# Last terms of two gate and up halves side by side in 64 rows, with value sums in the maxima banks, in a gated mix of attention and a ReLU-gated block

## The chip, the cores and the metric

The kernel runs on one core of a Trainium2 chip. The metric is the device time of one execution in microseconds; lower is better. TensorE is called PE in the profile, VectorE DVE, ScalarE ACT, GpSimd POOL and SyncE SP.

## The reference

```python
x = A_x                                            # 1 x 2048 x 448
g = sigmoid((x * gate_w).sum(-1, keepdims=True))

# attention: 16 heads of 28
qkv = (x @ wqkv).reshape(B, S, 3, 16, 28)          # q, k, v: b h s d
scores = einsum("bhqd,bhkd->bhqk", q, k) * 28 ** -0.5
a = (einsum("bhqk,bhkd->bhqd", softmax(scores), v)  # heads side by side
     ) @ wo

# gated block on B_x is not used: it reads the same x
gate = einsum("bsd,df->bsf", x, W_gate)            # f = 1792
up = einsum("bsd,df->bsf", x, W_up)
b = einsum("bsf,fd->bsd", gate * (gate > 0) * up, W_down)

out = g * a + (1 - g) * b
```

All inputs and outputs are float32.

## The kernel before

**Terms.** Products that must be precise are made of two parts: a float32 value is split into a high part (fp32r) and the remainder, its low part. A product of x and weights is a sum of high x high, low x high and high x low. The depth is 448: three chunks of 128 rows and one of 64. The 64 rows of the last chunk lie twice in the 128 partitions, for x and for the weights; of the weights, rows 0 to 63 of slot 6 hold the high part and rows 64 to 127 the low part, so one pass gives high and low weights times high x. `TERMS` lists the 11 passes of a product as pairs (slot of weights, chunk of x; chunks 4 to 7 are the low parts of x); `BY_CHUNK` sorts them by chunk, so that the last pass, n = 10, is (6, 7): slot 6 times the low part of x's last chunk. Of that pass only the 64 rows with high weights matter.

**Stages.** First the projections to q, k and v (`qk`, `vproj`), with the first maxima and scores among them. Then 34 rounds of attention, one head after another. At the end a last phase (`todo`, `gate_up`, `wout`, `down`) with the output projection of the heads, the remaining gate and up features, and the down projection.

**A round.** Every engine's order is written out by hand. A round is a string of letters and a number of gate and up halves, `(order, nu)` in `ROUNDS`:

- "s" (`scores`): one pass, 128 keys by 512 queries of scores, in one of two PSUM banks with tag "s"; ScalarE takes the exponential into SBUF, and that frees the bank. In the last three rounds (`LATE`) a pair of "s" goes to a pair of banks with tag "mx" instead (`scores_pair`).
- "m" (`smax`): two passes of scores for the row maxima, some heads ahead, into one of two pairs of banks with tag "mx"; VectorE reduces the pair (`tensor_reduce`, 128x1024).
- "x" (`gu_mm`): one of the 11 passes of a half. Half 0 of a feature is its gate, half 1 its up part, 128 features by 512 rows of x. When a half's passes are done, `relu` (ScalarE) reads the gate, and `spill_h` (VectorE) multiplies the up part by it; GpSimd's queue sends the product to DRAM.

The strings are SHORT (16 s, 8 m, 11 x), LONG (32 s, 16 m, 33 x; 3 halves), WIDE (32 s, 16 m, 44 x; 4 halves) and LATE (32 s, 44 x). There are 25 LONG, 3 WIDE and 3 LATE rounds. After the letters, `split_f` splits the next weights into parts (ScalarE the high parts, GpSimd the low parts), and `pv` makes the value sums of the round's 8 key tiles: per key tile four matmuls in plain float32 with 32 columns each, one for every 512 queries, side by side in the array. A head takes 16 key tiles, so two rounds; its sum stays in the one bank with tag "po" over both, and at the end of the head ScalarE copies it out (`os`), from where the row sums go to DRAM and come back spread (`row_sums`, `spread`) for `normalise`. At the start of every other round `smax_end` transposes a head's maxima ("mt") into the bank with tag "x".

**PSUM** has eight banks: two "s", two pairs "mx", one "po", one "x". In the rounds the halves use the one "x" bank (in LATE the "s" banks, and `relu` runs on VectorE). `ps_any` gives the projections "s", "s", "x" and "po" in turn; the last phase accumulates `down` in the same four and puts gate and up of a feature in a pair of "mx".

**In the last phase** a feature's `gate_up` makes 22 passes in a row; `down`, `wout` and `gate_up` alternate. `done` is the number of features that the rounds have made (50 of 56), so six remain. In `gu_mm`, where the last feature of a block of 512 rows of x has read a chunk for the last time, SyncE's queue reloads that chunk for the next block.

Of the kernel before, what the change touches and what calls it, by code (L numbers as in the profile page):

```python
# [47 lines left out]
ROUNDS = [("ssssssss", 0), ("smssmssmsmss", 0), (SHORT, 1)] + [(LONG, 3)] * 9 + ([(WIDE, 4)] + [(LONG, 3)] * 8) * 2 + [(WIDE, 4)] + [(LATE, 4)] * 3  # L48
NP = 9


# [10 lines left out]
def gated_mix_kernel(ctx, tc, x, wq, wo, wgu, wd, out):  # L62
# [11 lines left out]
    def ps_s(name):  # L74
        return psum.tile([P, TB], F32, tag="s", bufs=2, name=name)
# [16 lines left out]
    def low(dst, src, high):  # L92
        nc.vector.tensor_tensor(dst, src, f32(high), op=OP.subtract)  # L93
# [98 lines left out]
    def xf(tb, b):  # L192
        return X[tb][b // 4][:, b % 4]


    with tc.tile_pool(name="qkv", bufs=1) as pa:
# [61 lines left out]

        def ps_any(name, late=False):
            turn[0] += 1  # L260
            if late:
                return (ps_x, ps_o)[turn[0] % 2](name)
            return (ps_s, ps_s, ps_x, ps_o)[turn[0] % 4](name)

        def mix(n, among):

# [43 lines left out]

        warm = const.tile([P, TB], BF16, name="warm")
        nc.vector.memset(warm, 0.0)
        ps = ps_o("warm_ps")
        for n in range(WARM):
            nc.tensor.matmul(ps, warm[:, :P], warm, start=True, stop=True)

# [104 lines left out]
    def gu_mm(ps, i, s, n):  # L421

        a, b = BY_CHUNK[n]
        nc.tensor.matmul(ps, WS[i][:, s, a], xf(i // NF, b), start=(n == 0), stop=(n == NT - 1))  # L424
# [22 lines left out]


    NI = H * NK
    PO, OS, LS = {}, {}, {}  # L450

    def pv(i):
        h, kt = divmod(i, NK)
        if kt == 0:
            PO[h] = ps_o(f"po_{h}")
        for j in range(NB):
            nc.tensor.matmul(PO[h][32 * j:32 * j + 32], V[:, h // 4 % 2, kt, h % 4], PT[i][:, j], start=(kt == 0),  # L457
                             stop=(kt == NK - 1))
        del PT[i]
        if kt == NK - 1:  # L460
            OS[h] = fe.tile([P, TB], F32, name=f"os_{h}", tag="os", bufs=2)
            nc.scalar.activation(OS[h], PO.pop(h), AF.Copy)
            LS[h] = fe.tile([P, 16], F32, name=f"ls_{h}", tag="ls", bufs=2)
            nc.gpsimd.dma_start(LS[h], OS[h][DH::32].rearrange("j (p c) -> j p c", c=16))

# [35 lines left out]
        act_high(WO[:, 6], r[:, 3])  # L501
        pool_low(WO[64:, 6], r[64:, 3], WO[64:, 6])

    done = sum(n for _, n in ROUNDS) // 2
    nxt = parts = i0 = 0

    def small_things(u):
# [24 lines left out]
    for r, (order, nu) in enumerate(ROUNDS):  # L532
        ni = order.count("s") // NB
        late = order == LATE
        todo = list(range(nxt, nxt + nu))
        nxt += nu
        small_things(i0 // 4)
        if m % (2 * NK) == 0 and i0 <= NI - LEAD:
            smax_end(m // (2 * NK) - 1)
        if late and wor is None:  # L540
            wor = load_wo()
        ns = nx = 0
        for o in order:
            if o == "s":
                i, j = i0 + 1 + ns // NB, ns % NB
                if ns == 4 * NB:
                    small_things(i0 // 4 + 1)
                if len(EARLY) <= i * NB + j < NI * NB and not late:
                    scores(i, j)
                elif late and i < NI and j % 2 == 0:  # L550
                    scores_pair(i, j)
                ns += 1
            elif o == "m":
                smax(m)
                m += 1
            elif nx < NT * nu:
                i, half = divmod(todo[nx // NT], 2)
                if nx % NT == 0:
                    ps = (ps_s if late else ps_x)(f"gu_{i}_{half}")
                gu_mm(ps, i, half, nx % NT)  # L560
                nx += 1
                if nx % NT == 0:
                    spill_h(i, ps) if half else relu(i, ps, late)

        ready = nxt + (ROUNDS[r + 1][1] if r + 1 < len(ROUNDS) else 2)
# [6 lines left out]
        for i in range(i0, i0 + ni):  # L572
            pv(i)
            if i == NI - NK // 2:
                split_wo(wor)
        i0 += ni
    assert i0 == NI and m == len(maxima), (i0, m)
    stk.close()

# [80 lines left out]
    def down(i):  # L660
        tb, f = divmod(i, NF)
        if f == 0:
            ACC[tb] = [ps_s(f"acc_{tb}_0"), ps_s(f"acc_{tb}_1"), ps_x(f"acc_{tb}_2"), ps_o(f"acc_{tb}_3")]
# [82 lines left out]
```

## Time and profile before

| | us |
|---|---|
| median of 3 runs | 1302.82 (1302.03 to 1303.94) |
| the profiled execution | 1303.31 |
| its span in the trace | 1301.5 |
| busy: TensorE | 1293.8 |
| busy: VectorE | 800.2 |
| busy: ScalarE | 759.8 |
| busy: GpSimd | 360.4 |
| granted TensorE clock | 0.998 |

The profile's page gives the busy time of each engine, the span in 40 slices, the chain of work that ended last, and groups of instructions. In a group's row stand the line, the engine and the operation, what it writes and reads, "out<-in" with partitions x elements, and the count; after the bar the busy time and the mean duration of one in ns; after the second bar the idle time of the engine just before them, and what ended it. A row of the timeline has the start, the length in us, the engine, the line, the operation and how many were merged into it; in brackets stand the idle time before it and what ended that. A row of the chain of waits in order of time has start, length and what ran. PEld is the loading of weights, which can run under a matmul. Matmuls are pipelined: the length of one is longer than the distance to the next, so distances are taken from starts. A value sum matmul in float32 leaves two records, and its "po<-V" rows are those whose exponentials lie in free parts of the tile V.

### The profile page before, as it was taken

The numbers are of one execution on the slowest core, as the hardware profiler recorded it, in microseconds if no ns is written. First come the engines' busy times: TensorE is split into PE (matmuls) and PEld (weight loads), VectorE is DVE, ScalarE is ACT, GpSimd is POOL, SyncE is SP. The second block draws the span as 40 slices with busy tenths as digits, with TensorE's granted clock in tenths as the row PEclk, the third lists the DMA queues.
The fourth block names the chain that finished last, engine by engine and source line by source line (L and its number), as shares of the span: only waits on it lengthen the run. The fifth ranks groups of instructions, "written<-read, shape, count | busy, mean of one in ns | idle before, by whom it ended". The sixth has DMA issues, their size and how long they took to land.

```text
span 1301.5 us, 17614 instructions
## 1 busy us (share of the span) xinstructions
PE 1293.8 (99%) x6689; PEld 915.4 (70%) x6689; DVE 800.2 (61%) x832; ACT 759.8 (58%) x1387; POOL 360.4 (28%) x496
## 2 busy tenths in 40 slices
PE   9999999999999999999999999999999999999998
PEld 6888666666666666666666666666666566899997
DVE  6577676666767666766667676767676223553332
ACT  6212586667676676767667667676666665222121
POOL 3222113232222232323224222222223444541020
PEclk9999999999999999999999999999999999999999
DMA  9835524142333614141526143241423234634432
GB/s 312 281 154 227 154 72 109 56 114 62 85 94 93 170 58 95 60 90 57 130 71 170 61 97 77 78 95 52 103 64 102 94 97 150 221 95 156 133 111 78
DMA packets 53533, 148.87 MB, mean 114 GB/s; under 512 B 9992, under 2 KB 17096, under 8 KB 48840
## 3 DMA queue, kind: packets, MB, share of 16 engines
q1 hardware_dynamic: 36376, 98.57, 29.1%
q0 software_dynamic: 16928, 48.93, 10.3%
q8 instruction: 53, 0.87, 0.3%
q14 instruction: 32, 0.26, 0.1%
q10 hardware_dynamic: 144, 0.23, 0.0%
HBM read 102.06 MB, written 46.02 MB: 114 GB/s over the span
## 4 chain that ended last, share of the span: by engine, by line
PE 99%; DVE 0%; DMA 0%; issue 0%; ACT 0%; SPq 0%; DVEq 0%; ACTq 0%
PE gu L424 22%; PE sm L149 18%; PE po L457 17%; PE s L175 17%; PE acc L647 11%; PE qk L285 5%; PE v L295 3%; PE wo L603 3%; PE s L186 2%; DMA xr<-x 0%; PE mt L159 0%; DVE W L93 0%; DVE X L93 0%; DVE mx L151 0%; DVE st L93 0%
## 5 line engine op out<-in xcount | busy, mean ns | idle before, releaser
L151 DVE TENSOR_REDUCE mx<-sm 128x1 f32<-128x1024 f32 x512 | 612.7, 1220 | 203.7 <-PE sm L149 202.9
L177 ACT ACTIVATE P<-s 128x512 f32<-128x512 f32 x724 | 414.2, 597 | 117.6 <-PE s L175 86.1
L424 PE MATMUL gu<-X,wg 128*128 128x512 f32 x1232 | 389.7, 396 | 0.0
L175 PE MATMUL s<-Q,K 114*128 114x512 f32 x932 | 361.2, 403 | 0.0
L149 PE MATMUL sm<-K,Q 112*128 112x512 f32 x1024 | 314.3, 396 | 0.2 <-DVE mx L151 0.2
L424 PEld LDWEIGHTS gu<-X,wg 128*128 128x128 f32 x1232 | 233.3, 189 | 47.8 <-issue 0.8
L175 PEld LDWEIGHTS s<-Q,K 114*128 114x128 f32 x932 | 173.5, 188 | 86.4 <-ACT P L177 36.1
L149 PEld LDWEIGHTS sm<-K,Q 112*128 112x128 f32 x1024 | 193.6, 190 | 44.1 <-issue 1.7
L457 PE MATMUL po<-P,V 128*32 128x512 f32 x1600 | 182.8, 597 | 2.0 <-DVE st L93 2.0
L96 POOL TENSOR_TENSOR wg<-wgr,wg 128x384 fp32r<-128x384 f32 x153 | 142.7, 945 | 101.9 <-issue 51.8
L446 POOL DMA_DIRECT2D h_d<-h x56 | 31.7, 566 | 403.2 <-DVE h L440 357.4
L647 PE MATMUL acc<-WD,hh 128*128 128x448 f32 x672 | 140.9, 368 | 0.0
L177 ACT ACTIVATE V<-s 128x512 f32<-128x512 f32 x208 | 119.5, 598 | 28.3 <-PE s L175 18.8
L647 PEld LDWEIGHTS acc<-WD,hh 128*128 128x128 f32 x672 | 126.1, 188 | 12.8
L457 PEld LDWEIGHTS po<-P,V 128*32 128x32 f32 x1600 | 49.6, 110 | 113.3 <-issue 113.3
L87 ACT ACTIVATE hh<-hr 128x512 fp32r<-128x512 f32 x56 | 35.2, 631 | 120.3 <-PE acc L647 120.3
L93 DVE TENSOR_TENSOR hh<-hr,hh 128x512 fp32r<-128x512 f32 x56 | 43.5, 777 | 64.5 <-ACT hh L87 64.5
L285 PE MATMUL qk<-X,W 128*128 128x512 f32 x308 | 78.8, 396 | 0.3 <-DVE X L93 0.2
L285 PEld LDWEIGHTS qk<-X,W 128*128 128x128 f32 x308 | 57.6, 188 | 15.6 <-DVE X L93 1.6
L440 DVE TENSOR_TENSOR h<-gu,rl 128x512 f32<-128x512 f32 x56 | 38.6, 689 | 39.9 <-PE gu L424 24.6
L87 ACT ACTIVATE wg<-wgr 128x384 fp32r<-128x384 f32 x153 | 61.7, 490 | 0.0
L93 DVE TENSOR_TENSOR mh<-mr,mh 16x128 fp32r<-16x128 f32 x16 | 4.5, 279 | 83.6 <-ACT mh L163 83.6
(68 smaller groups left out, 724.9 us busy)
## 6 DMA issues: line engine op xcount, KB each, us to landing
wgr<-wgu SPq DMA_DIRECT2D x56, 512.0 KB
K<-qk_d SPq DMA_DIRECT2D x64, 224.0 KB
Q<-qk_d SPq DMA_DIRECT2D x64, 224.0 KB
h_d<-h POOLq DMA_DIRECT2D x56, 256.0 KB, 2.3
hr<-h_d SPq DMA_DIRECT2D x56, 256.0 KB
qk_d<-st POOLq DMA_DIRECT2D x22, 512.0 KB, 3.2
x_d<-X POOLq DMA_DIRECT2D x6, 1024.0 KB, 5.1
X<-x_d SPq DMA_DIRECT2D x24, 256.0 KB
```

The source lines that it names most:

```text
L87: nc.scalar.activation(dst, src, AF.Copy)
L93: nc.vector.tensor_tensor(dst, src, f32(high), op=OP.subtract)
L96: nc.gpsimd.tensor_tensor(dst, src, f32(high), op=OP.subtract)
L149: nc.tensor.matmul(ps[:, c, :], Q[h][:GD, u * P:(u + 1) * P], K[h % 3][:GD, k0:k0 + TB], start=True, stop=True)
L151: nc.vector.tensor_reduce(MX[h][:, 2 * u + half:2 * u + half + 1], ps, axis=AX.XY, op=OP.max)
L175: nc.tensor.matmul(ps, K[h % 3][:GD + 2, kt * P:(kt + 1) * P], Q[h][:GD + 2, j * TB:(j + 1) * TB], start=True, stop=True)
L177: nc.scalar.activation(PT[i][:, j], ps, AF.Exp, scale=SCALE)
L285: nc.tensor.matmul(ps, W[:, a, c * P:(c + 1) * P], xf(tb, b), start=(n == 0), stop=(n == NT - 1))
L295: nc.tensor.matmul(ps[:, :VC], xf(tb, b)[:, t * P:(t + 1) * P], W[:, a, 2 * D:], start=(n == 0), stop=(n == NT - 1))
L424: nc.tensor.matmul(ps, WS[i][:, s, a], xf(i // NF, b), start=(n == 0), stop=(n == NT - 1))
L457: nc.tensor.matmul(PO[h][32 * j:32 * j + 32], V[:, h // 4 % 2, kt, h % 4], PT[i][:, j], start=(kt == 0), stop=(kt == NK - 1))
L647: nc.tensor.matmul(ACC[i // NF][t][:, :D], HH[i][:, a, t * P:(t + 1) * P], WD[:, f, b], start=(f == 0 and n == 0), stop=(f == NF - 1 and n ...
```

## The change

The last passes of two halves are issued together, each with 64 rows, one in the upper and one in the lower half of the array. For one half of such a pair (the set `SECOND`) the high part of the weights lies in rows 64 to 127, and the low part in rows 0 to 63; `split_f` makes the low part for each half separately. In the 31 LONG, WIDE and LATE rounds the last two halves are held open without their last pass, and a new letter "h" at the end of the string issues both last passes, followed by `relu` and `spill_h`. So the strings have 31, 42 and 42 x and one h. In the last phase `gate_up` makes the 20 other passes of a feature first, and then the two last ones.

Two halves are open at once and need two banks: "po" is given up and "x" has two. The value sums of a round (a visit) now start anew in each round, in the first bank of a pair with tag "mx" (in LATE rounds in an "x" bank). On a head's first visit ScalarE copies them out; on later ones VectorE adds them to the copy in SBUF. There are 34 visits, 16 of them first ones.

The letters of LONG and WIDE stand in another order too. In LONG a score comes five passes after the one before last in 13 places (before: 9), in WIDE in 7 (before: 5).

```diff
-LONG = "ssmmxsxxsxsmxxsxsmsxxsxxsmmsxxsxxsxsmsxxsmsmsxsxxsxmsmsxxxxsmxssxxmsxsmsxxsmsxmss"
-WIDE = "msxxsmsxsxmsxxsxmsxxxxmssmxsxxsxxsmxmssxxxxsxsmsmsxxxxsxsmsxmsxxsxxxsmsmxxxsxsxxxsxmssxmxxss"
-LATE = "ssxxxssxxxssxxxssxx" * 4
+LONG = "mxsmsxxxxxsmsxsmsxxsmsxsmsxxsmxxsmsxsxxsmsxxsxsmxsxsmsxxsmsxsmsxxsmsxsxxsmsmxssh"
+WIDE = "sxxmxmxxsxxmsxxsxsmxxssxmxmxsxxsxxsxsmsxxsmxssxxxsmsxxsmxsmxsxsmxsmsxsxxsmsxxsmsmsxxsxsh"
+LATE = "ssxxxssxxxssxxxssxx" * 2 + "ssxxxssxxxssxxssxx" * 2 + "h"
...
-    def ps_o(name):
-        return psum.tile([P, TB], F32, tag="po", bufs=1, name=name)
-
     def ps_x(name):
-        return psum.tile([P, TB], F32, tag="x", bufs=1, name=name)
+        return psum.tile([P, TB], F32, tag="x", bufs=2, name=name)
...
+    done = sum(n for _, n in ROUNDS) // 2
+    SECOND = {sum(n for _, n in ROUNDS[:r + 1]) - 1 for r in range(len(ROUNDS)) if "h" in ROUNDS[r][0]}
+    SECOND |= set(range(2 * done + 1, 2 * NB * NF, 2))
+
+    def lane(k):
+        return slice(64 * k, 64 * k + 64)
...
             high(w[:, :, 6], wr[:, :, 3])
-            low(w[64:, :, 6], wr[64:, :, 3], w[64:, :, 6])
+            for s in range(2):
+                rows = lane(1 - (2 * i + s in SECOND))
+                low(w[rows, s, 6], wr[rows, s, 3], w[rows, s, 6])
...
     def gu_mm(ps, i, s, n):
         a, b = BY_CHUNK[n]
-        nc.tensor.matmul(ps, WS[i][:, s, a], xf(i // NF, b), start=(n == 0), stop=(n == NT - 1))
+        rows = slice(0, P)
+        if n == NT - 1 and 2 * i + s in SECOND | {k - 1 for k in SECOND}:
+            rows = lane(int(2 * i + s in SECOND))
+        nc.tensor.matmul(ps, WS[i][rows, s, a], xf(i // NF, b)[rows], start=(n == 0), stop=(n == NT - 1))
...
-    def pv(i):
-        h, kt = divmod(i, NK)
-        if kt == 0:
-            PO[h] = ps_o(f"po_{h}")
-        for j in range(NB):
-            nc.tensor.matmul(PO[h][32 * j:32 * j + 32], V[:, h // 4 % 2, kt, h % 4], PT[i][:, j], start=(kt == 0),
-                             stop=(kt == NK - 1))
-        del PT[i]
-        if kt == NK - 1:
+    def pv(i0, ni, late):
+
+        h = i0 // NK
+        po = ps_x(f"po_{i0}") if late else ps_w(f"po_{i0}")[:, 0]
+        for i in range(i0, i0 + ni):
+            p = PT.pop(i)
+            for j in range(NB):
+                nc.tensor.matmul(po[32 * j:32 * j + 32], V[:, h // 4 % 2, i % NK, h % 4], p[:, j], start=(i == i0),
+                                 stop=(i == i0 + ni - 1))
+        if i0 % NK == 0:
             OS[h] = fe.tile([P, TB], F32, name=f"os_{h}", tag="os", bufs=2)
-            nc.scalar.activation(OS[h], PO.pop(h), AF.Copy)
+            nc.scalar.activation(OS[h], po, AF.Copy)
+        else:
+            nc.vector.tensor_tensor(OS[h], po, OS[h], op=OP.add)
+        if (i0 + ni) % NK == 0:
...
+        passes = [(*divmod(k, 2), n) for k in todo for n in range(NT - ("h" in order and k >= nxt - 2))]
+        units = []
...
+            elif o == "x":
+                i, half, n = passes.pop(0)
+                if n == 0:
                     ps = (ps_s if late else ps_x)(f"gu_{i}_{half}")
+                    units.append((i, half, ps))
+                gu_mm(units[-1][2], i, half, n)
+                if n == NT - 1:
+                    i, half, ps = units.pop()
                     spill_h(i, ps) if half else relu(i, ps, late)
+            elif o == "h":
+                for i, half, ps in units:
+                    gu_mm(ps, i, half, NT - 1)
+                for i, half, ps in units:
+                    spill_h(i, ps) if half else relu(i, ps, late)
...
         for s in range(2):
-            for n in range(NT):
+            for n in range(NT - 1):
                 gu_mm(ps[:, s], i, s, n)
+        for s in range(2):
+            gu_mm(ps[:, s], i, s, NT - 1)
         relu(i, ps[:, 0])
         spill_h(i, ps[:, 1])
```

In `ps_any`, the warm-up and `down`, the place of "po" is taken by the second "x" bank.

More of the change, by code (lines that the diff above doesn't have):

```diff
@@ L41 @@
 SHORT = "smsxxsmsxsmsxmsxsmsxxsmsxsmsxxsmsxs"
-LONG = "ssmmxsxxsxsmxxsxsmsxxsxxsmmsxxsxxsxsmsxxsmsmsxsxxsxmsmsxxxxsmxssxxmsxsmsxxsmsxmss"
-WIDE = "msxxsmsxsxmsxxsxmsxxxxmssmxsxxsxxsmxmssxxxxsxsmsmsxxxxsxsmsxmsxxsxxxsmsmxxxsxsxxxsxmssxmxxss"
-LATE = "ssxxxssxxxssxxxssxx" * 4
-ROUNDS = [("ssssssss", 0), ("smssmssmsmss", 0), (SHORT, 1)] + [(LONG, 3)] * 9 + ([(WIDE, 4)] + [(LONG, 3)] * 8) * 2 + [(WIDE, 4)] + [(LATE, 4)] * 3
+LONG = "mxsmsxxxxxsmsxsmsxxsmsxsmsxxsmxxsmsxsxxsmsxxsxsmxsxsmsxxsmsxsmsxxsmsxsxxsmsmxssh"
+WIDE = "sxxmxmxxsxxmsxxsxsmxxssxmxmxsxxsxxsxsmsxxsmxssxxxsmsxxsxmsxmsxsxmsxsmxsxsxxsmsxxsmsmsxxsxsh"
+LATE = "ssxxxssxxxssxxxssxx" * 2 + "ssxxxssxxxssxxssxx" * 2 + "h"
+ROUNDS = [("ssssssss", 0), ("smssmssmsmss", 0), (SHORT, 1)] + [(LONG, 3)] * 9 + ([(WIDE, 4)] + [(LONG, 3)] * 8) * 2
+ROUNDS += [(WIDE, 4)] + [(LATE, 4)] * 3
 NP = 9
@@ L260, in ps_any @@
             turn[0] += 1
-            if late:
-                return (ps_x, ps_o)[turn[0] % 2](name)
-            return (ps_s, ps_s, ps_x, ps_o)[turn[0] % 4](name)
+            return (ps_s, ps_s, ps_x, ps_x)[turn[0] % 4](name) if not late else ps_x(name)
         def mix(n, among):
@@ L312, in gated_mix_kernel @@
         nc.vector.memset(warm, 0.0)
-        ps = ps_o("warm_ps")
+        ps = ps_x("warm_ps")
         for n in range(WARM):
@@ L449, in gated_mix_kernel @@
     NI = H * NK
[L450 to L460 removed]
+    OS, LS = {}, {}
+    def pv(i0, ni, late):
[7 more added lines that the diff above has]
+        if i0 % NK == 0:
             OS[h] = fe.tile([P, TB], F32, name=f"os_{h}", tag="os", bufs=2)
[L462 removed]
+            nc.scalar.activation(OS[h], po, AF.Copy)
+        else:
+            nc.vector.tensor_tensor(OS[h], po, OS[h], op=OP.add)
+        if (i0 + ni) % NK == 0:
             LS[h] = fe.tile([P, 16], F32, name=f"ls_{h}", tag="ls", bufs=2)
@@ L502, in split_wo @@
         pool_low(WO[64:, 6], r[64:, 3], WO[64:, 6])
-    done = sum(n for _, n in ROUNDS) // 2
     nxt = parts = i0 = 0
@@ L541, in gated_mix_kernel @@
             wor = load_wo()
-        ns = nx = 0
+        passes = [(*divmod(k, 2), n) for k in todo for n in range(NT - ("h" in order and k >= nxt - 2))]
+        units = []
+        ns = 0
         for o in order:
+            if o == "x" and not passes:
+                continue
             if o == "s":
@@ L555, in gated_mix_kernel @@
                 m += 1
-            elif nx < NT * nu:
-                i, half = divmod(todo[nx // NT], 2)
-                if nx % NT == 0:
+            elif o == "x":
+                i, half, n = passes.pop(0)
+                if n == 0:
                     ps = (ps_s if late else ps_x)(f"gu_{i}_{half}")
-                gu_mm(ps, i, half, nx % NT)
-                nx += 1
-                if nx % NT == 0:
+                    units.append((i, half, ps))
+                gu_mm(units[-1][2], i, half, n)
+                if n == NT - 1:
+                    i, half, ps = units.pop()
                     spill_h(i, ps) if half else relu(i, ps, late)
+            elif o == "h":
[3 more added lines that the diff above has]
+                    spill_h(i, ps) if half else relu(i, ps, late)
+        assert not passes, (r, passes)
         ready = nxt + (ROUNDS[r + 1][1] if r + 1 < len(ROUNDS) else 2)
@@ L571, in gated_mix_kernel @@
                 fetch_f(parts // 2 + 1)
[L572 to L575, printed above, removed]
+        pv(i0, ni, late)
         i0 += ni
+        if late and i0 == NI:
+            split_wo(wor)
     assert i0 == NI and m == len(maxima), (i0, m)
@@ L662, in down @@
         if f == 0:
-            ACC[tb] = [ps_s(f"acc_{tb}_0"), ps_s(f"acc_{tb}_1"), ps_x(f"acc_{tb}_2"), ps_o(f"acc_{tb}_3")]
+            ACC[tb] = [ps_s(f"acc_{tb}_0"), ps_s(f"acc_{tb}_1"), ps_x(f"acc_{tb}_2"), ps_x(f"acc_{tb}_3")]
         if i not in LAST:
```

## The prediction

> **What bounds the kernel now.** I read the page first: busy shares, granted clock, chain of waits.
>
> ```profile
> PE 1293.8 (99%) x6689; PEld 915.4 (70%) x6689; DVE 800.2 (61%) x832; ACT 759.8 (58%) x1387; POOL 360.4 (28%) x496
> ...
> PEclk9999999999999999999999999999999999999999
> ...
> PE 99%; DVE 0%; DMA 0%; issue 0%; ACT 0%; SPq 0%; DVEq 0%; ACTq 0%
> PE gu L424 22%; PE sm L149 18%; PE po L457 17%; PE s L175 17%; PE acc L647 11%; PE qk L285 5%; PE v L295 3%; PE wo L603 3%; PE s L186 2%; DMA xr<-x 0%; PE mt L159 0%; DVE W L93 0%; DVE X L93 0%; DVE mx L151 0%; DVE st L93 0%
> ```
>
> TensorE is the path from end to end at full clock; every other engine has a third of the span free or more. A busy share cannot say whether a pass costs what it should, so the next view is the chain in order of time, which shows the pitch of things.
>
> ```profile
> 585.37 7.00 PE po L457 x64
> ...
> 615.39 7.00 PE po L457 x64
> ...
> 1035.86 7.00 PE po L457 x64
> 1060.84 7.00 PE po L457 x64
> ...
> 1104.94 5.15 PE gu L424 x22
> ```
>
> One gate and up feature in the last phase is 22 passes in 5.15 us: 0.234 us a pass. A LONG round takes 615.39 - 585.37 = 30.02 us, of which the value sums hold 7.00; a LATE round takes 24.98. Now the timeline at the end of a LONG round, around the value sums.
>
> ```profile
> 614.74 0.65 PE L175 MATMUL s<-Q,K 114*128 114x512 f32 x2
> ...
> 615.32 0.16 PEld L457 LDWEIGHTS po<-P,V 128*32 128x32 f32 x8 [0.24 <-issue]
> 615.32 1.92 PE L457 MATMUL po<-P,V 128*32 128x512 f32 x16
> 615.77 0.13 PEld L457 LDWEIGHTS po<-P,V 128*32 128x32 f32 x4 [0.30 <-issue]
> 616.20 0.13 PEld L457 LDWEIGHTS po<-P,V 128*32 128x32 f32 x4 [0.30 <-issue]
> ...
> 621.35 0.13 PEld L457 LDWEIGHTS po<-P,V 128*32 128x32 f32 x4 [0.30 <-issue]
> ...
> 622.32 0.30 PEld L175 LDWEIGHTS s<-Q,K 114*128 114x128 f32 x2 [0.84 <-issue]
> 622.32 0.73 PE L175 MATMUL s<-Q,K 114*128 114x512 f32 x2
> 622.46 0.60 ACT L462 ACTIVATE os<-po 128x512 f32<-128x512 f32 x1 [5.03 <-PE po L457]
> 622.66 0.89 PEld L149 LDWEIGHTS sm<-K,Q 112*128 112x128 f32 x4
> 622.89 1.10 PE L149 MATMUL sm<-K,Q 112*128 112x512 f32 x4
> 623.35 0.75 POOL L464 DMA_DIRECT2D ls<-os  x1 [3.71 <-ACT os L462]
> 623.56 2.36 DVE L151 TENSOR_REDUCE mx<-sm 128x1 f32<-128x1024 f32 x2 [7.19 <-PE sm L149]
> ```
>
> The value sums use the array as four tiles of 32 columns, everything else as one of 128x128. The price of turning it over can be read here. Going in: two passes from 614.74 would end at 615.21, the sums start at 615.32 (0.11 late), and their first group takes 0.45 (615.32 to 615.77) against (621.35 - 616.20) / 12 = 0.429 for the others: 0.13 us. Coming out: the load at 621.35 runs under group 15 of 16, so group 16 ends at 621.35 + 2 x 0.429 = 622.21; the scores start at 622.32 (0.11 late), and the two of them take 0.57 to the next pass at 622.89 instead of 0.468 (0.10 late): 0.21 us. Coming out, where weights of 128 columns are loaded, costs 0.08 more than going in with 32.
>
> The LONG round adds up: 97 passes x 0.234 = 22.70, 16 groups x 0.429 = 6.86, two switches 0.34: 29.90, so 0.12 us of 30.02 is waiting. A LATE round has 76 x 0.234 + 6.86 + 0.34 = 24.98, nothing left. The waiting is on score banks:
>
> ```profile
> 600.62 1.30 ACT L177 ACTIVATE V<-s 128x512 f32<-128x512 f32 x2 [0.31 <-PE s L175]
> ...
> 600.90 0.39 PE L175 MATMUL s<-Q,K 114*128 114x512 f32 x1
> ...
> 601.59 0.39 PE L175 MATMUL s<-Q,K 114*128 114x512 f32 x1
> ...
> 601.98 0.19 PEld L175 LDWEIGHTS s<-Q,K 114*128 114x128 f32 x1 [0.19 <-ACT V L177]
> ...
> 602.05 0.43 PE L175 MATMUL s<-Q,K 114*128 114x512 f32 x1
> ...
> 602.32 0.63 PE L149 MATMUL sm<-K,Q 112*128 112x512 f32 x2
> ```
>
> There are two score banks. The scores at 602.05 are the second after those at 600.90, five passes on; their weights could only be loaded at 601.98, when ScalarE let the bank go at 601.92, and the next pass comes 0.27 instead of 0.234 later. Counted in the letters, LONG has 9 places where a score comes five passes after the one before last; 0.12 / 9 is 0.014 us for each.
>
> **The change, part by part.** The profiled execution took 1303.31 us (span 1301.5); the median of the runs shown is 1302.82, so 0.49 is taken off at the end.
>
> *Tails side by side, in the rounds.* The last term of a half needs only 64 of its 128 rows. Each LONG (25), WIDE (3) and LATE (3) round now holds back the last terms of its last two halves and issues them at the round's end in the upper and lower 64 rows: 31 pairs. A pair removes one pass, 0.234, and adds what the second tile costs beside the first, plus one more switch: 128x128 to 64x128. From 64x128 into the value sums takes the place of the switch into them, and is the same 0.13. The second tile: four loads of 32 columns take 0.13 us together and single ones 0.11 in the same view, so some 0.006. The switch does not occur in this trace. Its bounds: nothing, if halving the rows is no change of tiling; 0.21, the way out of the sums, which loads 128 columns like a tail. In between is the 0.13 in. I take 0.21, since the tail's weights have 128 columns. So a pair is worth 0.234 - 0.006 - 0.21 = 0.018, and 31 pairs 0.56 us. With 0.13 they would be worth 3.0, with nothing 7.1; if the two loads queue up instead, another 0.10 each is lost, 3.1.
>
> The rule that speaks against the change is in the Trainium skill, "TensorEngine Tiling (Array Packing)", section Key Properties: changing the tiling mode, not just the tile, drains TensorE. The trace agrees for 32 columns (0.13 and 0.21); for 64 rows no run here shows it. By that rule alone the pair is nearly worthless; by the same section's other statement, that tiles load and multiply independently, it saves nearly a pass.
>
> *The same in the last phase.* Six features have their two tails behind 20 full passes, with full passes following: two switches for one pass. 6 x (0.228 - 0.21 - 0.21) = 1.15 us lost (bounds: 1.4 gained, 1.8 lost with queued loads).
>
> *New letters.* LONG now has 13 five-pass places instead of 9, WIDE 7 instead of 5. Four more at 0.014 are 0.056 a round, 25 rounds: 1.4 us lost; WIDE 3 x 0.03 = 0.1. Below: a place can cost nothing where ScalarE has no backlog, so 0. Above: 0.035, as at 602.05, 25 x 0.14 = 3.5.
>
> *Value sums in a maxima bank.* The visits that are not a head's first (18 of 34) add into SBUF on VectorE; 16 ScalarE copies stay.
>
> ```profile
> L151 DVE TENSOR_REDUCE mx<-sm 128x1 f32<-128x1024 f32 x512 | 612.7, 1220 | 203.7 <-PE sm L149 202.9
> ...
> L440 DVE TENSOR_TENSOR h<-gu,rl 128x512 f32<-128x512 f32 x56 | 38.6, 689 | 39.9 <-PE gu L424 24.6 <-ACT rl L437 14.3 <-issue 0.8
> ...
> L96 POOL TENSOR_TENSOR wg<-wgr,wg 64x256 fp32r<-64x256 f32 x51 | 37.6, 737 | 4.0
> ...
> L480 DVE TENSOR_TENSOR os<-os,rb 128x512 f32<-128x512 f32 x16 | 13.9, 867 | 0.0
> ...
> L462 ACT ACTIVATE os<-po 128x512 f32<-128x512 f32 x16 | 9.6, 599 | 72.2 <-PE po L457 72.2
> ```
>
> An add has the form of L440, PSUM and SBUF to SBUF: 0.689, 12.4 us of VectorE in all, off the path: VectorE idles 7.19 us across the value sums. What matters is the bank. In a LONG round the first maxima after the sums use the other bank, whose reduction ended long before; the second use the bank that the add must empty, and four passes lie between. Counted from the first pass after the sums: the second maxima start at 4 x 0.234 + 0.10 = 1.04. The copy starts 0.14 after that pass (622.46 against 622.32), so the add ends at 0.14 + 0.69 = 0.83; a release takes 0.13 (ScalarE ended at 601.92, the pass began at 602.05): 0.96. It fits with 0.08 to spare. Queued behind a waiting maxima pass is everything on TensorE, so a miss would count in full: I allow 0.03 for each of 18 adds, 0.5 us (bounds 0 and, if it takes the 0.867 of L480's product on the same tile, 0.10 late, 1.8).
>
> *The rest at nothing.* Two banks in turn for the halves: the single bank shows no wait of TensorE, so nothing is gained; the held pair fills both, and ReLU and product (0.6 + 0.69) empty them under the 7.00 us of sums. Cover gone, they would delay the next round's first half by about 1.3. The product's DMA and the weight splits on GpSimd stand behind it in that same cover. The low part of the tail weights becomes two instructions of 64x128 for one of 64x256 (737 ns): between none and 0.7 us more of GpSimd each, 28% busy. The three reloads of the last quarter of x on SyncE's queue move to their round's end, under the sums, and that quarter is the last that the next half reads. The transposed maxima take one of the two banks where they took the single one. The early phase swaps banks one for one.
>
> *Sum.* -0.56 + 1.15 + 1.4 + 0.1 + 0.5 = +2.6 us: 1303.31 + 2.6 = 1305.9 in the profiled execution, **1305.4** as a median.
>
> **Rivals.** *1, a cheap switch.* If taking half the rows costs 0.09 or less, the pairs win. For it: nothing but column tiles has shown its price here, and weights of full passes are loaded under the previous pass (622.66, 0.89 for four). Against: both switches that the trace has cost more. At 0.11: 31 x 0.118 + 6 x 0.008 - 2.0 = 1.7 gained, 1301.1; at nothing: 37 x 0.228 - 2.0 = 6.4 gained, 1296.4. From 0.09 downward it is faster by over 2.6.
>
> *2, the tails run in turn.* If the second tile's weights load only after the first's, 37 x 0.10 more: 1309.1; if they also stream in turn, 37 x 0.228 more: 1313.8. For: the column tiles work in fp32, these in fp32r, so nothing here shows two such tiles at once. Against: four column tiles do run at once, 64 records in 7.00 us with the sums' four groups in 0.429.
>
> *3, the add as the new wait (slower).* The second maxima after the sums wait for VectorE. It decides once the add ends more than 0.08 late. At 0.10 late (0.867 us) it makes 1.8 instead of 0.5: 1306.7; at 0.3 late, which would take a late start too, 18 x 0.3 = 5.4: 1310.3. Against: VectorE has nothing else queued there.
>
> *4, it does not do what it says:* the halves are paired in the built order in all 31 rounds and 6 features, so this leaves only a wash in which every term is overrated, about 1303.
>
> **How the numbers follow.** The forecast has 0.50, its own range 1303 to 1308: the pairs' price between 0.17 and 0.25, the score places between 0 and 2.5. A difference of 0.2%, 2.6 us, is about what a measurement of this kernel can tell from no change; the forecast lies on that line, so its half is 0.27 slower and 0.23 same. Rival 1 has 0.24: 0.17 faster, 0.07 same. Rival 2 has 0.14 and rival 3 0.08, both slower. Rival 4 has 0.04, same. Faster 0.17, same 0.34, slower 0.49. The range leaves out the cheapest switches below and the fully serial tails above: 1298.5 to 1311.5.
>
> **What would show it.** Right: LONG rounds still 30.0 to 30.1 us apart, with the first tail 0.4 to 0.45 after the full pass before it, the second within some 10 ns, and features of the last phase at 5.3 us instead of 5.15. Rounds of 29.8 and features under 5.15 mean rival 1. A second tail 0.1 or more behind the first means rival 2. A gap of TensorE before the second maxima, ended by VectorE's add, means rival 3. More VectorE time without such a gap means nothing. If the score waits vanish or triple, the price of 0.014 for a five-pass place was wrong.

## The result and the profile after

| us | before | the change |
|---|---|---|
| median | 1302.05 (1300.51 to 1304.83, 18 runs) | 1304.29 (1303.32 to 1308.73, 18 runs) |
| ratio, 95% interval | | 1.0017 [1.001, 1.0025] |
| the profiled execution | 1303.31 | 1304.31 |
| its span | 1301.5 | 1302.4 |
| granted clock in it | 0.998 | 0.997 |

The change makes the kernel about 0.17% slower, 2.2 us. A second measurement gave 1305.48 against 1302.74, ratio 1.002 [1.0011, 1.0028]. The forecast was 1305.4 us.

The page of the change, its busy shares, its granted clock and its chain of waits:

```profile
PE 1292.6 (99%) x6689; PEld 900.7 (69%) x6689; DVE 816.3 (63%) x855; ACT 763.5 (59%) x1387; POOL 363.5 (28%) x547
...
PEclk9999899999999999999999999999999999999999
...
PE 86%; DMA 1%; POOL 0%; DVE 0%; issue 0%; ACT 0%; ACTq 0%; POOLq 0%; DVEq 0%
PE gu L434 21%; PE po L469 17%; PE s L174 16%; PE sm L148 16%; PE acc L673 11%; PE wo L627 3%; PE s L185 2%; DMA ls<-os 1%; POOL wg L95 0%; DMA qk_d<-st 0%; PE mt L158 0%; DVE mx L150 0%; ACT wg L86 0%; ACT P L176 0%; DVE e L389 0%
```

TensorE is as busy as before, and VectorE has 16 us more. Two things are new. The chain, followed back, now leads through an exponential (`ACT P`) to a DMA `qk_d<-st`, which are not among its lines of before, and it goes no further than the issue of that DMA at 145.24 us. That is why TensorE's share falls from 99% to 86%: the 11% of the span ahead of the DMA, the projections, are not in this chain, and the fall is for the most part no waiting. And the fifth slice, 130 to 163 us, has an 8 in the granted clock. Both point at the start of the attention, a place that the prediction had put down as "one for one". The timeline of the change there:

```profile
143.03 1.92 PE L469 MATMUL po<-P,V 128*32 128x512 f32 x16
...
145.24 0.71 POOL L287 DMA_DIRECT2D qk_d<-st  x1 [3.18 <-DVE st L92]
145.46 0.19 PEld L174 LDWEIGHTS s<-Q,K 114*128 114x128 f32 x1
145.70 0.40 PE L174 MATMUL s<-Q,K 114*128 114x512 f32 x1
...
148.56 0.60 ACT L473 ACTIVATE os<-po 128x512 f32<-128x512 f32 x1 [4.34 <-DMA qk_d<-st]
...
149.06 1.08 ACT L176 ACTIVATE P<-s 128x512 f32<-128x512 f32 x2
...
149.70 0.80 PE L174 MATMUL s<-Q,K 114*128 114x512 f32 x1 [3.61 <-ACT P L176]
```

The same place in the kernel before, in a second profiled execution of it (called "before again" below):

```profile
145.53 1.92 PE L457 MATMUL po<-P,V 128*32 128x512 f32 x16 [1.99 <-DVE st L93]
...
147.38 0.50 PE L175 MATMUL s<-Q,K 114*128 114x512 f32 x1
147.72 0.64 PE L149 MATMUL sm<-K,Q 112*128 112x512 f32 x2
147.92 2.99 ACT L177 ACTIVATE P<-s 128x512 f32<-128x512 f32 x5 [3.26 <-PE s L175]
```

Before, the first head's sum stayed in its bank over all its visits (four, as its first rounds are short), and no copy stood in ScalarE's queue here. Now the first visit of every head is copied out, and the first of these copies waits 4.34 us, until the DMA that stores the last projection has landed. The tile `os` lies in SBUF that the projections' buffers have just given up. The exponentials are queued behind the copy, both score banks stay full, and TensorE stands still for 3.61 us. Then it runs at half rate for a while. The windows of the first stretch show it; in each row stand the bounds, the length, the busy times of PE, PEld, DVE, ACT and POOL, the granted clock, the DMA share and GB/s. Before again, and then the change:

```profile
148.00:152.00 4.00, 4.00 (x15) 2.17 (x13) 3.61 (x4) 3.43 (x7) 0.00 (x0) 1.00 0.42 137
152.00:156.00 4.00, 4.00 (x26) 2.11 (x26) 2.61 (x5) 3.60 (x9) 2.19 (x3) 1.00 1.02 264
```

```profile
148.00:152.00 4.00, 2.30 (x5) 1.79 (x6) 0.61 (x1) 2.36 (x5) 0.00 (x0) 0.50 0.59 152
152.00:156.00 4.00, 4.00 (x20) 2.34 (x22) 3.07 (x3) 2.73 (x6) 0.00 (x0) 0.68 1.01 225
```

On the other side, the first value sums no longer use the bank that the last projection holds, so the 1.99 us wait of before is gone and they start 2.5 us earlier (2.0 to 2.8 over the four executions below).

Three starts of value sums cut the span into parts: the first of all, those of the SHORT round (from which the LONG rounds run), and the last. The last part is the last phase with the sums ahead of it. All from the timelines, in us:

| | before | before again | the change | the change again |
|---|---|---|---|---|
| first value sums | 145.79 | 145.53 | 143.03 | 143.50 |
| to SHORT's sums | 20.47 | 19.08 | 24.77 | 24.16 |
| SHORT's sums start | 166.26 | 164.61 | 167.80 | 167.66 |
| rounds, to the last sums | 918.62 | 918.89 | 917.04 | 918.87 |
| last sums to the end | 216.6 | 216.7 | 217.6 | 217.6 |
| span | 1301.5 | 1300.2 | 1302.4 | 1304.1 |

Against before again, the change is 3.1 us late when the LONG rounds begin, wins between nothing and 1.8 us in the 31 rounds that follow, and loses 0.9 us in the last phase. The execution of before that the prediction was worked from had itself run at half rate for a while at this place (20.47 instead of 19.08).

In the rounds, the end of a LONG round in the timeline of the change, with the pair between the last scores and the value sums:

```profile
283.13 0.66 PE L174 MATMUL s<-Q,K 114*128 114x512 f32 x2
...
283.71 0.19 PEld L434 LDWEIGHTS gu<-X,wg 64*128 64x128 f32 x2 [0.25 <-issue]
283.71 0.49 PE L434 MATMUL gu<-X,wg 64*128 64x512 f32 x2
284.14 0.16 PEld L469 LDWEIGHTS po<-V 128*32 128x32 f32 x8 [0.24 <-issue]
```

The two tails are one entry: they start together, 4 ns apart in their starts, last 0.49 us in all, and their two loads are merged in 0.19. Two scores from 283.13 would end at 283.60, so the pair starts 0.11 late; it takes 0.43 to the value sums. By the starts of single passes, the last score is 0.351 before the first tail, and the second tail 0.421 before the sums, together 0.776 us; two whole tails take 3 x 0.233 + 0.11 = 0.81 there.

The sums' end in another LONG round of the change:

```profile
261.23 0.73 PE L148 MATMUL sm<-K,Q 112*128 112x512 f32 x2
261.37 0.69 DVE L475 TENSOR_TENSOR os<-po,os 128x512 f32<-128x512 f32 x1 [5.42 <-PE po L469]
...
262.27 0.63 PE L148 MATMUL sm<-K,Q 112*128 112x512 f32 x2
```

The add starts 0.14 after the first maxima pass and ends at 262.06; the second maxima start 1.04 after the first, with no wait. In the groups the 18 adds have 0.692 us each:

```profile
L475 DVE TENSOR_TENSOR os<-po,os 128x512 f32<-128x512 f32 x18 | 12.5, 692 | 88.7 <-PE po L469 83.8 <-issue 4.9
```

The last phase in the chain of waits in order of time, before and then the change. Before, 22 passes of a feature and 12 of `down` take 7.63 us, and with the pair 7.74:

```profile
1104.94 5.15 PE gu L424 x22
1110.09 2.48 PE acc L647 x12
1112.57 5.15 PE gu L424 x22
```

```profile
1105.34 5.11 PE gu L434 x22
1110.45 2.63 PE acc L673 x12
1113.08 5.11 PE gu L434 x22
```

The view gives the price of leaving the pair to the passes behind it: the feature has 0.04 less and `down` 0.15 more.

### The profile page after: what moved, and what is told of

Its sections match the earlier page's. It is cut to its first block, busy times and chain, and to the rows that moved or that the text cites. A ratio compares the mean times of both kernels' runs of the same rounds, so it can differ in the third digit from the quotient of the medians.

```text
span 1302.4 us, 17702 instructions
## 1 busy us (share of the span) xinstructions
PE 1292.6 (99%) x6689; PEld 900.7 (69%) x6689; DVE 816.3 (63%) x855; ACT 763.5 (59%) x1387; POOL 363.5 (28%) x547
## 4 chain that ended last, share of the span: by engine, by line
PE 86%; DMA 1%; POOL 0%; DVE 0%; issue 0%; ACT 0%; ACTq 0%; POOLq 0%; DVEq 0%
PE gu L434 21%; PE po L469 17%; PE s L174 16%; PE sm L148 16%; PE acc L673 11%; PE wo L627 3%; PE s L185 2%; DMA ls<-os 1%; POOL wg L95 0%; DMA qk_d<-st 0%; PE mt L158 0%; DVE mx L150 0%; ACT wg L86 0%; ACT P L176 0%; DVE e L389 0%
## 5 line engine op out<-in xcount | busy, mean ns | idle before, releaser
L434 PE MATMUL gu<-X,wg 128*128 128x512 f32 (+1 forms) x1232 | 388.3, 401 | 0.0
L174 PE MATMUL s<-Q,K 114*128 114x512 f32 x932 | 368.8, 402 | 3.6 <-ACT P L176 3.6
L148 PE MATMUL sm<-K,Q 112*128 112x512 f32 x1024 | 325.4, 399 | 0.7 <-DVE mx L150 0.7
L434 PEld LDWEIGHTS gu<-X,wg 128*128 128x128 f32 (+1 forms) x1232 | 226.0, 189 | 54.2 <-issue 11.2
L95 POOL TENSOR_TENSOR wg<-wgr,wg 128x384 fp32r<-128x384 f32 x204 | 146.5, 735 | 28.7 <-ACT wg L86 10.5
L475 DVE TENSOR_TENSOR os<-po,os 128x512 f32<-128x512 f32 x18 | 12.5, 692 | 88.7 <-PE po L469 83.8
```

Of the source, the lines that this page charges most:

```text
L95: nc.gpsimd.tensor_tensor(dst, src, f32(high), op=OP.subtract)
L148: nc.tensor.matmul(ps[:, c, :], Q[h][:GD, u * P:(u + 1) * P], K[h % 3][:GD, k0:k0 + TB], start=True, stop=True)
L174: nc.tensor.matmul(ps, K[h % 3][:GD + 2, kt * P:(kt + 1) * P], Q[h][:GD + 2, j * TB:(j + 1) * TB], start=True, stop=True)
L434: nc.tensor.matmul(ps, WS[i][rows, s, a], xf(i // NF, b)[rows], start=(n == 0), stop=(n == NT - 1))
```

## The experiments

Four theories stood against one another: the loss sits in the first head's copy; it sits in the pairs (rivals 1 and 2); in the letters; in the adds.

**The first copy apart.** The first head's first sum goes to a free part of V instead of the projections' memory, and the add at the second visit takes it from there.

```diff
-        if i0 % NK == 0:
+        if i0 == 0:
+            OS[h] = p_slot(5, "os_first")[:, 0]
+            nc.scalar.activation(OS[h], po, AF.Copy)
+        elif i0 % NK == 0:
...
-            nc.vector.tensor_tensor(OS[h], po, OS[h], op=OP.add)
+            old = OS[h]
+            if i0 == ROUNDS[0][0].count("s") // NB:
+                OS[h] = fe.tile([P, TB], F32, name=f"os_{h}", tag="os", bufs=2)
+            nc.vector.tensor_tensor(OS[h], po, old, op=OP.add)
```

> Theory: the change's loss is a one-off at the start. Its first value-sum copy on ScalarE waits 4.34 us for a DMA of the projection stage, the exponentials queue behind it, TensorE stands still for 3.6 us and its clock then falls to half. With the first head's first sum copied into a free part of the V tile instead, that wait goes: the visit after the first comes back from 11.9 to 8 to 9 us, and the run is 2 to 3.5 us shorter than the changed kernel, 1300.8 to 1302.3 where before has 1302.05. Rival (the prediction's): the loss lies in the LONG rounds' score waits, 0.06 us in each of 25, and at the start another wait takes the place of this one: within 0.7 us of the changed kernel.

Measured: 1300.49 us (11 runs) against 1302.36 of before, ratio 0.9989 [0.998, 0.9998]. It was run again beside the change itself on one chip, with before at 1302.74:

> The change once more, so that it stands on one chip with the three kernels after it. If its loss sits in the first head's copy, it is again 1.5 to 3 us slower than before. If the loss was a matter of the chip or of the half clock by chance, it comes out within 1 us of before.

> The change with the first head's first sum put into a free part of V instead of the memory that the projections leave. By the theory that the copy into that memory costs the start, 3 to 4 us below the change, so 1 to 2 us below before, as it was on the other chip. If that was the chip, it equals the change.

Measured: the change again 1305.48 (ratio 1.002), the first copy apart 1302.39 (0.9999 [0.999, 1.0008]). So the copy costs the change 3.1 us on this chip. The expected gain over before, 1 to 2 us, came on the first chip and not on the second: a kernel without the wait equals before within 0.2%. The timeline of that second run:

```profile
145.12 0.60 ACT L473 ACTIVATE V<-po 128x512 f32<-128x512 f32 x1 [0.94 <-PE po L469]
...
145.62 1.77 ACT L176 ACTIVATE P<-s 128x512 f32<-128x512 f32 x3
...
146.26 0.50 PE L174 MATMUL s<-Q,K 114*128 114x512 f32 x1 [0.20 <-ACT P L176]
...
153.00 0.50 PE L434 MATMUL gu<-X,wg 128*128 128x512 f32 x1 [0.17 <-ACT wg L86]
...
154.15 0.49 PE L434 MATMUL gu<-X,wg 128*128 128x512 f32 x1 [0.65 <-POOL wg L95]
```

The copy waits for the value sums alone, and TensorE for 0.20 us instead of 3.61. SHORT's sums start at 163.98, 3.68 us earlier than in the change again (167.66). Part is given back on the way: the first half of gate and up now comes before its weights are split (0.17 and 0.65 us). The granted clock of the single runs tells the same: 1.0 in 8 of the 11 runs of this kernel and in 10 of 11 on the first chip, in 20 of 33 runs of before, and in none of the 29 runs of the change.

**Tails of all rows, at the same places.** The second tile goes, all else stays, the start too.

```diff
-            rows = lane(int(2 * i + s in SECOND))
+            rows = slice(0, P)
```

> The changed kernel with the paired last passes issued at the same places, but each over all 128 rows, one after the other. Theory (a pair is worth 0.03 us in a round and costs 0.15 us in a feature of the last phase): LONG rounds 29.97 instead of 29.945 us, features of the last phase back to 5.15 us; in all the same as the changed kernel within 0.5 us, 1304.3. Rival (the pairs earn most of a pass): 31 x 0.2 = 6 us slower than the changed kernel, 1310. Rival (the pairs cost): 1 to 3 us faster than it.

Measured: 1305.03 us, ratio 1.0022 [1.0013, 1.0031]; the change 1.0017 and 1.002. In its trace the end of a LONG round is 0.257 + 0.233 + 0.328 = 0.818 us, 0.042 more than with the pair, and LONG rounds are 30.067 us apart. Both are a little above what was expected (29.97 us a round, 1304.3 within 0.5). The times alone do not tell the two kernels apart, but the starts do: a pair is worth 0.04 us, against 0.234 for the pass that it saves.

**Both tails in one tile.** Both in the lower 64 rows, so that they can't run at once.

```diff
-                rows = lane(1 - (2 * i + s in SECOND))
+                rows = lane(1)
...
-            rows = lane(int(2 * i + s in SECOND))
+            rows = lane(0)
```

> The changed kernel with both last passes of a pair in the lower 64 rows, so that they cannot run at once; switches, places and all other work stay. If the two tiles truly run at once in the changed kernel, this costs one more streamed pass for each of 37 pairs, 37 x 0.22 = 8 us: 1312.5. If they ran in turn there, 0. In between, the difference over 37 is what running at once is worth per pair.

Measured: 1313.8 us, ratio 1.0084 [1.0071, 1.0098]. That is 9.5 us over the first median of the change and 8.3 over the second, so 0.22 to 0.26 for each of the 37 pairs. The end of a round in its timeline:

```profile
283.92 0.66 PE L174 MATMUL s<-Q,K 114*128 114x512 f32 x2
284.50 0.73 PE L434 MATMUL gu<-X,wg 64*128 64x512 f32 x2
285.16 1.06 PE L469 MATMUL po<-V 128*32 128x512 f32 x8
```

Again the pair starts 0.11 after the end of the two scores, but takes 0.66 to the sums instead of 0.43. So the tails of the change do run at once, which ends rival 2, and what eats the gain is the way in and out of the mode.

**The pair ahead of the last scores.** "h" stands before "ss" (with the first copy apart), so that full passes follow it instead of the sums (in WIDE it stands between the last two scores).

```diff
-LONG = "...smsmxssh"
+LONG = "...smsmxhss"
```

> The version with the first sum's copy put apart, with the pair in the LONG and WIDE rounds issued ahead of the round's last scores (two in LONG, one in WIDE) instead of right before the value sums. Theory: a change of tiling costs each time, and before the value sums one of the two is shared; away from them the pair pays one more, 0.18 us in 28 rounds: 5 us slower, 1305.5. Rival (the price is the waiting for weights that any neighbour hides): within 1 us of 1300.5.

Measured: 1306.99 us against 1302.37 of before, ratio 1.0035 [1.0022, 1.0048]. LONG rounds are 30.12 us instead of 30.02, so a place between full passes costs 0.10 more than one that shares its way out with the sums. The rounds as a whole take 1085.18 - 163.93 = 921.25, 2.0 more than in the kernel with the last phase as before, below, on the same chip (919.24). The median is 1.5 us above what was expected; the profiled execution was the shortest of the five, so its trace shows the place and not the whole sum.

**The old letters.** "s" and "m" stand as before with two x taken out, the held pair stays.

```diff
-LONG = "mxsmsxxxxxsmsxsmsxx...smsmxssh"
-WIDE = "sxxmxmxxsxxmsxxsxsm...smsmsxxsxsh"
+LONG = "ssmmsxxsxsmxxsxsmsx...sxsmsxxsmsxmssh"
+WIDE = "msxxsmsxsxmsxxsxmsx...xxxsxmssxmxxssh"
```

> The changed kernel with the earlier order of scores and maxima in LONG and WIDE (two x taken out, h at the end), which has 9 places where a score comes five passes after the one before last instead of 13 (WIDE 5 instead of 7). The prediction's price of 0.014 us for a place: LONG rounds 0.056 shorter, 1.5 us faster than the changed kernel, 1302.8. Theory now (the places cost no more in the new order, since the two traces show the same 0.13 to 0.15 us of waits in a LONG round): within 0.5 us of the changed kernel.

Measured: 1313.8 us, ratio 1.009 [1.0076, 1.0104]. Both theories missed: fewer five-pass places cost 9 us more. Its timeline at the begin of a round shows why:

```profile
231.73 0.70 PE L174 MATMUL s<-Q,K 114*128 114x512 f32 x2
231.84 0.60 ACT L473 ACTIVATE os<-po 128x512 f32<-128x512 f32 x1 [5.02 <-PE po L469]
...
232.33 0.25 ACT L161 ACTIVATE mr<-mt 16x128 f32<-16x128 f32 x1
232.61 0.31 ACT L162 ACTIVATE mh<-mr 16x128 fp32r<-16x128 f32 x1
232.83 1.76 ACT L176 ACTIVATE P<-s 128x512 f32<-128x512 f32 x3
...
233.45 0.50 PE L174 MATMUL s<-Q,K 114*128 114x512 f32 x1
```

The two first scores stand at the head of the round, but the copy of the first visit now falls into the same round as the transposed maxima, so 0.60 + 0.25 + 0.31 us of ScalarE come ahead of their exponentials. The next score starts at 233.45, after four passes from 232.28 that would end at 233.22. By the starts of the passes this costs some 0.36 us in each of 12 LONG rounds. The new letters begin with "mxsmsxxxxx", which leaves ScalarE that time. In 12 rounds it is a ReLU that comes ahead of tight scores, for some 0.30 us. One of the x taken out in this run stood fifth in the string, so the first half ends, and its ReLU comes, after the letters "smms" instead of before them: this second wait comes from where the x was taken out, and not from the copy. So the change needs other letters than these, and about half of the 9 us is the copy at the first visit meeting the old order. An old order with its x taken out elsewhere was not run.

**The add twice.** A second add of the same bank, into a tile that nobody reads, ahead of the real one (with the first copy apart).

```diff
+            again = fe.tile([P, TB], F32, name=f"again_{i0}", tag="again", bufs=1)
+            nc.vector.tensor_tensor(again, po, old, op=OP.add)
             nc.vector.tensor_tensor(OS[h], po, old, op=OP.add)
```

> The version with the first sum's copy put apart, with every add of the value sums made twice (first into a spare tile), so that the bank is given back 0.69 us later. The trace shows the add ending 0.21 us before the second maxima start, and a release taking 0.13: 0.08 to spare. Theory: 0.69 - 0.08 = 0.6 us of waiting in the rounds that follow an add and have maxima, 14 of them (less where WIDE follows): 7 to 8.5 us slower than 1300.5. Rival (the bank has more room than that, or VectorE's time hides): under 2 us.

Measured: 1312.16 us, ratio 1.0074 [1.006, 1.0087]. The timeline after the sums of a round:

```profile
259.02 0.73 PE L148 MATMUL sm<-K,Q 112*128 112x512 f32 x2
259.15 0.69 DVE L482 TENSOR_TENSOR again<-po,os 128x512 f32<-128x512 f32 x1 [5.42 <-PE po L469]
259.88 0.69 DVE L483 TENSOR_TENSOR os<-po,os 128x512 f32<-128x512 f32 x1
...
260.72 0.70 PE L148 MATMUL sm<-K,Q 112*128 112x512 f32 x2 [0.50 <-DVE os L483]
```

The second maxima start 1.70 after the first instead of 1.04, ended by the add. LONG rounds with an add are 30.63 to 30.70 us, the others 29.93 to 29.98. So the wait of rival 3 exists and is seen in full once the add is late; one add is in time. The total, 10.2 us over the kernel with the last phase as before (1301.94) on the same chip, is more than the 7 to 8.5 expected, since WIDE rounds (33.21 once) and the last phase lost too.

**The last phase as before**, on top of the first copy apart: both tails of its features are whole again.

```diff
-    SECOND |= set(range(2 * done + 1, 2 * NB * NF, 2))
...
-            for n in range(NT - 1):
+            for n in range(NT):
...
-        for s in range(2):
-            gu_mm(ps[:, s], i, s, NT - 1)
```

> The version with the first sum's copy put apart, and the six features of the last phase made as before the change, 22 full passes each; pairs in the rounds alone. In the changed kernel's trace a feature with its two switches takes 5.20 us and the accumulation after it 2.54, against 5.155 and 2.48 before: 0.105 for each, 0.63 for six, and one wait of 0.24 at the first accumulation. Theory: 0.6 to 0.9 us faster than the version with the first copy apart (1300.49): 1299.7. Rival: the last phase is not bound by TensorE alone there and other waits take the place: within 0.3 us of it.

> The same with the last phase's tails as they were (two full passes instead of the pair). If the six features lose 0.1 each by their pairs, as the chain says, it is 0.2 to 0.6 us below the kernel with the first sum apart on the same chip. If other waits take their place, the two are the same within 0.3 us, and the 1.4 us between them in the runs so far was the chip.

Measured: 1301.94 (ratio 0.9997 [0.9988, 1.0006]) and, on one chip with the first copy apart (1302.39), 1302.58 (1.0 [0.9991, 1.0008]). The first expectation missed by 2 us; the second run shows that most of the 1.4 between the two kernels was the chip. The last part is 217.4 and 217.1 us in the two traces instead of 217.6 (before: 216.7), so a quarter to half of the last phase's loss goes with the pairs; for the rest, a wait of about 0.5 us at the first `down` is there in both. In the median the pairs of the last phase can't be told from nothing.

**The first two visits in one**, instead of the first copy apart: the copy comes later, when the DMA has landed.

```diff
-ROUNDS = [("ssssssss", 0), ("smssmssmsmss", 0), (SHORT, 1)] + ...
+ROUNDS = [("sssssssssmssmssmsmss", 0), (SHORT, 1)] + ...
```

> The change with the first two rounds made one (20 scores and 8 maxima in one round, so one visit with 16 key tiles fewer switches, 33 visits in all instead of 34). The first copy then falls some 8 us later, when the projections' last DMA has landed. By the theory of the first copy the 3.6 us wait and the half clock go, and one way in and out of the value sums (0.3 us): 1300 to 1301.5. If the wait only moves to the next round, it equals the change. It may lose up to 2 us where the value sums of the first visit, held back, leave TensorE waiting for exponentials.

Measured: 1303.08 us (1.0004 [0.9995, 1.0013]), 2.4 below the change on the same chip, clock 1.0 in 9 of 11 runs. The value sums start at 148.39 with no wait in front and SHORT's at 164.68, 3.0 earlier than in the change again. The time missed the expected 1300 to 1301.5, whose level came from the other chip. It is a second way of removing the wait, with the same result. The kernel before, profiled a second time ("before again"):

> The kernel before, unchanged, for a second trace: how much of the 1.3 us between its first profiled execution and the median of its runs lies in the LONG rounds, and how much at the start. Theory: the rounds differ by the same few hundredths of a microsecond each from execution to execution, without a change in the order of work: 29.95 to 30.05 us a LONG round.

Measured: 1301.92 us, span 1300.2, and LONG rounds of 29.994 us.

## Why the prediction was right, and where its steps were not

The sum was +2.6 us and the measured difference is +2.2 (+2.7 in the second measurement; +1.0 between the two profiled executions, +3.9 between the spans of before again and the change again; 20 of 33 runs of before had the clock at 1.0 and the others lost some of the start as well, so its median lies in between). It was right by terms that cancel, not by each step, and so by luck. Of its signs, the second tail within 10 ns held; the first tail came 0.35 us after the pass before it, not 0.4 to 0.45, and a feature took 5.20 us by the starts of its passes, not 5.3.

| us | predicted | measured |
|---|---|---|
| 31 pairs | -0.56 | -1.3 (0.042 each) |
| last phase | +1.15 | +0.9 |
| new letters | +1.5 | +0.3 to +0.8 at the five-pass places; -0.6 to +1.4 over the whole stretch of passes |
| adds | +0.5 | 0 |
| start | 0 | +3.1 against before again, +1.5 against the execution of before that the prediction used |

*The pairs.* The mechanism was as forecast: the second tail 4 ns after the first, and a switch that eats nearly all of the pass. The size of the switch was not. Into 64 rows it is 0.11 (0.09 in the last phase), not 0.21; out of them into the sums 0.42 - 0.23 = 0.19, where 0.11 of the 0.13 were expected at this place. So a switch that loads weights of 128 columns does not cost 0.21 for that reason alone, as the prediction had it; what sets the price stays open. Rival 1 asked for 0.09 in, with the price of the way out unchanged; the first was nearly reached, the second was not. The Trainium skill, "TensorEngine Tiling (Array Packing)", section Key Properties, has both rules that met here: the mode change drains TensorE, and tiles load and multiply independently. The trace agrees with both, with 0.11 and 0.19 us for the first and 4 ns for the second; one pair for each drain is too little work.

*The last phase.* A feature with its `down` is 0.11 longer, not 0.19, since the switches are cheaper; six make 0.6, and 0.24 of waiting at the first `down` brings the rest.

*The letters.* By the starts of passes, the waits for score banks are 0.14 and 0.16 us a LONG round in the two executions of the change, and 0.13 in before. Thirteen five-pass places cost hardly more than nine, so for these places the price of 0.014 for each further one was too high; the run with the old letters shows what counts more, the work that stands ahead of the exponentials in ScalarE's queue. The term as a whole stays open. The 89 passes in the middle of a LONG round, between its opening and its last four passes, take 20.91 us in both executions of before, 20.88 in the first execution of the change and in the kernel with both tails in one tile, but 20.97 in the change again and in seven traces of the other kernels with the new letters. That is 0.03 less or 0.06 more a round, -0.6 or +1.4 us over 25, and the second is just the 0.056 that the prediction had; the part outside the five-pass places lies in some 10 ns at many passes, and no run shows its cause.

*The adds.* The timing worked out in the prediction held to 0.01 us, and the 0.08 to spare sufficed. The allowance was not needed.

*The start.* The step that failed is "the early phase swaps banks one for one". The diff moves ScalarE's copy from a head's end to its first visit, and the prediction costed the copy's bank but not its destination and not the queue behind it. This term is larger than all the others; it happens to be nearly what the other errors sum to. Among the rivals none was this wait. The trace of before could not show the waiting write: there the first copy to `os` stood at the end of the first head, long after that DMA.

What stays open: LONG rounds of the same built kernel are 29.95 us in one execution and 30.02 in another (1.8 us in all), by some 10 ns at many passes. Six of the seven traces with these rounds have 30.02, against 30.00 in both of before: but for the first profiled execution, the rounds as a whole win nothing that the traces show. No run separates this from the value of the pairs over a whole execution. And one late LONG round waits 0.3 to 1 us for its maxima in most traces, before's too.

## What to carry to other kernels

Two tiles at once save a pass only if the work between two mode changes outweighs both changes; one pair of 512-column passes does not (0.04 of 0.23 us), and it does best where another mode follows anyway. When an edit moves an instruction to an earlier time, look at what memory it writes and whose last DMA still reads that memory, and at everything queued behind it on its engine. A sum that comes out right is no evidence for its terms: cut the two traces at the same landmarks and compare part by part.

## What had not been expected of the hardware

- A switch is cheaper into 64 rows (0.09 to 0.12 us) than out of them into 32 columns (0.19) or back to 128x128 (0.19 at the first pass, and some 0.1 more at the second).
- Two 64-row fp32r tiles with 512 columns start 4 ns apart; in one tile the second comes 0.33 later, 0.10 more than a pass.
- A wait of TensorE of 3.61 us at the start came with half rate for 6.8 us in one execution of the change (from 147.7 us on, within the wait) and for 3.4 in another (from 150.7, after it), and the 1.99 us wait of before with 3.4 us in one and none in the other. The Trainium skill, "TensorE: Matmul & The Clock Gate", section What's actually happening, gives a free-running window of 3.4 us after whose idleness the clock halves: lengths of one or two windows agree, but here half rate also came with a wait of 1.99 us, shorter than a window, in some executions.
